# Blockwise attention into a maxout layer on one core: another order of loads, and M computed during batch 0's exps

## The chip, the core and the metric

The kernel runs on one core of one Trainium2 chip. A core has a tensor engine (PE, with its weight loads shown as PEld), a vector engine (DVE), a scalar engine (ACT), GpSimd (POOL) and a sync engine (SP). Each runs its own instructions in order and waits for others by semaphores; 16 DMA engines move data between memory and the on-chip buffer. The metric is the device time of one execution in microseconds, as a median over runs.

## The reference

The input is q, k and v, each 8 batches x 8 heads x 576 positions x 64 in fp32, and three weights. Attention is causal by blocks of 64 positions; its output goes through a layer that takes the larger of two products.

```python
scores = scale * np.matmul(q, k.transpose(0, 1, 3, 2))
mask = (pos[:, None] // 64) >= (pos[None, :] // 64)
attn = softmax(np.where(mask, scores, -1e9))
x = np.matmul(attn, v)            # -> 4608 tokens x 512
g = np.maximum(x @ w1, x @ w2)    # w1, w2: 512 x 1024
out = g @ w_out                   # w_out: 1024 x 512
```

## The kernel before

The maxout is rewritten: max(x w1, x w2) = relu(x (w1 - w2)) + x w2. So the kernel needs D = w1 - w2 (`d_sb`, made by `diff_w`, one fp32 subtraction on DVE for each quarter of 256 columns), h = relu(x D), and M = w2 w_out (`m_sb`), and then out = h w_out + x M. For M, w2 has to be transposed: `bT_unit` does two blocks of 128 columns by eight PE transposes and one copy on DVE into `bT_sb`, and `m_unit` does one of eight 128 x 256 pieces of M by eight matmuls and one copy on DVE.

Attention runs over 32 pairs of heads, four for each batch. Two pairs make a group g; q and k come by group (`load_qk`, fp32, from SP's queue), are cast to bf16 (`cast`, by POOL from the third group on), transposed on PE (`transposes`) and copied out by DVE and ACT. A load that is "gated" is preceded by a tiny memset of POOL on the same buffer, so that SP issues it only when POOL has come to that place in its program. V, w1, w2 and w_out are loaded by POOL's own DMA queue; those to bf16 are cast on the way. w2 is put into stretches of the buffer xT that later batches' x will fill. w1 and w2 are loaded in four quarters each.

Scores go to two PSUM buffers (`ps_s`), ACT takes their exps into `aT`, POOL clears the masked corners (`mask`), and `av` multiplies by V with a column of ones and normalises on DVE (a reciprocal and a multiplication). `x_out` transposes the result into xT. All other PE results share four PSUM buffers (`ps_m`).

The order is written out by hand. Batch 0 (groups 0 and 1, pairs 0 to 3) is cut into small score tiles, `burst_p`, `burst_q1`, `burst_q2`, `burst_q3`, and its av is done in two parts, tiles [0, 1] and [2, 3, 4]. Then comes group 2 (pairs 4 and 5) by `tile_0`, `tile_1`, `tile_2`, each with its exps and masks in `region`, and from group 3 on a loop. Between these stand `fill(n)`, which issues the next steps of a list of units made by `plan()`: h, M, B-transposes and y (the output product, whose PSUM result is copied by DVE for the first two spans of tokens and by ACT later). `fill` counts in matmuls of 512 columns: a transpose step counts 0.25, an M step 0.5, an h step 0.5 in the first span (256 tokens), 0.625 in the second (320 tokens), and a y step 1. In and after the block that closes group 2, `fill_of(g)` spreads what is ready, less 6, over the groups that are left until new tokens come (three groups at g = 2, two at 3, one at 4). `warm_up(n)` issues n matmuls on zeros whose results are not used.

In the list before, a B-transpose unit follows every second h unit of the first span, and M comes after the second span's h.

Each engine's order is that of the program, so a DMA issue of POOL, a cast or a mask delays whatever POOL has to do after it, and a subtraction on DVE delays the copies and relus behind it.

Of the kernel before, what the change touches and what calls it, by code (L numbers as in the profile page):

```python
# [8 lines left out]
FP32 = mybir.dt.float32  # L9
# [5 lines left out]
def kernel(  # L15
# [10 lines left out]
    nc = tc.nc  # L26
# [85 lines left out]
    def load_qk(g, queues, gated=False):  # L112
        b, u = divmod(g, GPB)
        for nm, src, queue in (("q", q, queues[0]), ("k", k, queues[1])):
            if queue is None:
                continue
            raws[nm, g] = t = raw.tile([P, 2, RPP * D], FP32, name=f"{nm}raw")
            if gated:
                nc.gpsimd.memset(t[:, 0, :1], 0.0)
            queue.dma_start(  # L120
                out=t[:],
                in_=src[b, 4 * u:4 * u + 4].rearrange(
                    "(s h) (p t) d -> (h p) s (t d)", h=2, t=RPP),
            )

    def cast(nm, g, parts):
        t = raws[nm, g].rearrange("p s (t d) -> p t s d", d=D)
        if (nm, g) not in qk_n:
            qk_n[nm, g] = qkn.tile([P, RPP, 2, D], BF16, name=f"{nm}n")
        n = qk_n[nm, g]  # L130
        for copy, j0, j1 in parts:
            copy(out=n[:, j0:j1], in_=t[:, j0:j1])  # L132

    def load_v(b, c):
        rows = min(P, S - c * P)
        nc.gpsimd.dma_start(  # L136
            out=vv_r[b % NV][P - rows:, c, :, :D],
            in_=v[b, :, c * P:c * P + rows, :].rearrange("h p d -> p h d"),
        )
# [3 lines left out]
    wor = moe_w_out.rearrange("(c p) f -> p c f", p=P)  # L143

    WB = 256
    w1_raw, w2_sb = {}, []
    for j in range(d_ff // WB):
        row, n = (1, j) if j < 3 else (3, 0)
        t0 = 3 * S - 3 * BLK + n * NDM * WB
        w2_sb.append(xT[:, row, t0:t0 + NDM * WB].rearrange("p (c f) -> p c f", c=NDM))  # L150

    def load_w(j, which=(0, 1)):
        fs = slice(j * WB, (j + 1) * WB)
        if 0 in which:
            w1_raw[j] = wraw.tile([P, NDM, WB], FP32, name="w1raw")
            nc.gpsimd.dma_start(out=w1_raw[j][:], in_=w1r[:, :, fs])
        if 1 in which:
            nc.gpsimd.dma_start(out=w2_sb[j], in_=w2r[:, :, fs])

    def diff_w(j):  # L160
        fs = slice(j * WB, (j + 1) * WB)
        nc.vector.tensor_sub(d_sb[:, :, fs], w1_raw[j][:], w2_sb[j])  # L162

    WH = d_model // 2

    def load_wo(i):
        ds = slice(i * WH, (i + 1) * WH)
        nc.gpsimd.dma_start(out=wo_sb[:, :, ds], in_=wor[:, :, ds])  # L168
# [8 lines left out]
    nc.vector.memset(zeros[:], 0.0)  # L177
    nc.scalar.activation(out=warm[:], in_=warm[:], func=AF.Exp)
    load_qk(1, (SP, SP))
    load_qk(2, (SP, None))  # L180
    make_identity(nc, ident)
    for r in range(NV):
        nc.vector.memset(vv_r[r][:, :, :, D:D + 1], 1.0)
# [6 lines left out]
    cast("k", 0, ((act, 0, 5), (dve, 5, RPP)))  # L190
    for c in range(2):
        load_v(0, c)
    load_w(0, (0,))
    cast("q", 1, ((pool, 7, RPP),))
    cast("k", 1, ((pool, 0, 7),))
    load_w(0, (1,))


    done_tokens = [0]
# [23 lines left out]
    def bT_unit(j):  # L223
        pt = ps_m.tile([P, 2, NDM, P], BF16, name="ps_bT", tag="m")
        for i in range(2):
            for c in range(NDM):
                nc.tensor.transpose(pt[:, i, c, :], w2_sb[j][:, c, i * P:(i + 1) * P], ident[:])
                if i == 1 and c == NDM - 1:
                    nc.vector.tensor_copy(
                        out=bT_sb[:, 2 * j:2 * j + 2, :],  # L230
                        in_=pt.rearrange("p i c d -> p i (c d)"))
                yield

    def m_unit(i, c):
        ds = slice(i * WH, (i + 1) * WH)
        pt = ps_m.tile([P, WH], FP32, name="ps_M", tag="m")
        for f in range(NFF):
            nc.tensor.matmul(  # L238
                pt[:], bT_sb[:, f, c * P:(c + 1) * P], wo_sb[:, f, ds],
                start=(f == 0), stop=(f == NFF - 1),  # L240
            )
            if f == NFF - 1:
                nc.vector.tensor_copy(out=m_sb[:, c, ds], in_=pt[:])
            yield
# [40 lines left out]
    def plan():  # L285
        def h(i, f):
            t0, w = spans[i]
            units.append((h_unit(i, f), t0 + w, w / SPAN, NDM))

        def y(i, s, last=False):  # L290
            t0, w = spans[i]
            if last:
                units.append((y_last(i, s), t0 + w, 0.333, 3 * NY))
            else:
                units.append((y_unit(i, s), t0 + w, 1.0, NY))

        for i in range(NSPAN):
            for f in range(NFF):
                h(i, f)
                if i == 0 and f % 2:  # L300
                    units.append((bT_unit(f // 2), 0, 0.25, 2 * NDM))
                if i > 2 and f % 2 == 0 and f // 2 < tiles[i - 1]:
                    y(i - 1, f // 2)
            if i == 1:
                for n in range(2 * NDM):
                    units.append((m_unit(n // NDM, n % NDM), 0, 0.5, NFF))
                for j in range(2):
                    for s in range(tiles[j]):
                        y(j, s)
        n = tiles[-1]  # L310
        for s in range(n):
            y(NSPAN - 1, s, s == n - 1)
# [21 lines left out]
    def warm_up(n):  # L334
        pw = ps_m.tile([P, SPAN], FP32, name="ps_w", tag="m")
        for _ in range(n):
            nc.tensor.matmul(pw[:], zeros[:, :P], zeros[:], start=True, stop=True)  # L337
# [4 lines left out]
    def transposes(nm, g, copies):  # L342
        n = qk_n.pop((nm, g))
        pts = [ps_m.tile([P, RPP, NP], BF16, name=f"ps_{nm}T", tag="m") for _ in range(2)]
        for j in range(RPP):
            for i in range(2):
                r = slice(i * NP, (i + 1) * NP)
                nc.tensor.transpose(  # L348
                    pts[i][:, j, :], n[r, j].rearrange("p s d -> p (s d)"), ident[r, r],
                )  # L350

        def copy_out(which=(0, 1), part=(0, NP), copy=None):
            p0, p1 = part
            for i in which:
                t = (qT_r if nm == "q" else kT_r)[(2 * g + i) % NT]
                (copy or copies[i])(  # L356
                    out=t[:, p0 * RPP:p1 * RPP].rearrange("q (p j) -> q p j", j=RPP),
                    in_=pts[i][:, :, p0:p1].rearrange("q j p -> q p j"),
                )
        return copy_out  # L360
# [12 lines left out]
    def pad_keys(p):  # L373
        nc.gpsimd.tensor_copy(
            out=kz_r[p % NT].rearrange("p (a c) -> p a c", c=BLK)[:, 0:3:2],
            in_=kT_r[p % NT][:, S - 3 * BLK:].rearrange("p (a c) -> p a c", c=BLK)[:, 0:3:2],
        )
# [31 lines left out]
    def burst_q1(p):  # L409
        burst(p, ((0, QCUT, 320), (1, QCUT, 192)), 384)  # L410

    def burst_q2(p):
        burst(p, ((1, 448, P), (2, QCUT, 320), (4, 512, BLK)), 896)
# [4 lines left out]
    def masks_p(p, eng=None):  # L418
        for a in (0, 256):
            mask(p, a, eng)  # L420

    def masks_q(p, eng=None):
        for a in (1024, 1408):
            mask(p, a, eng)
# [30 lines left out]
    def region(*tiles):  # L455
        for out in tiles:
            out()
# [127 lines left out]
    burst_p(1)  # L585
    warm_up(2)
    masks_p(1)
    for c in range(2, NCH):
        load_v(0, c)
    load_qk(2, (None, SP), gated=True)  # L590
    load_w(1)
    cq = transposes("q", 1, (dve, dve))
    burst_q1(0)
    ck = transposes("k", 1, (dve, dve))
# [15 lines left out]
    masks_p(3, nc.vector)  # L610
    burst_q2(0)
    av(2, [0, 1])
    warm_up(2)
    x_out(0, 0, 2, (act, act))
    av(3, [0, 1])
    diff_w(0)
    burst_q1(1)
    warm_up(2)
    cast("q", 2, ((pool, 0, RPP),))
    masks_q(0)  # L620
    load_w(2)
    burst_q2(1)
    x_out(1, 0, 2)
    warm_up(2)
    burst_q3(1)
    masks_q(1)
    load_w(3)
    fill(4)
    burst_q1(2)
    transposes("q", 2, (dve, act))()  # L630
    burst_q2(2)
    av(0, [2, 3, 4])
    burst_q3(2)
    masks_q(2)
    cast("k", 2, ((pool, 0, RPP),))
    load_wo(0)
    load_wo(1)
    av(1, [2, 3, 4])
    burst_q1(3)
    burst_q2(3)  # L640
    av(2, [2, 3, 4])
    transposes("k", 2, (dve, act))()
    burst_q3(3)
    masks_q(3)
    pad_keys(4)
    pad_keys(5)
    for c in range(NCH):
        load_v(1, c)
    load_qk(3, (SP, SP), gated=True)
    x_out(0, 2, NCH)  # L650
    fill(2)
    diff_w(1)
    outs = tile_0(4), tile_1(4)
    av(3, [2, 3, 4])
    region(*outs)
    x_out(1, 2, NCH)
    fill(4)
    diff_w(2)
    fill(2)
    region(tile_2(4), tile_0(5))  # L660
    fill(4)
    diff_w(3)
    fill(2)
    region(tile_1(5), tile_2(5))
    fill(4)
    fill(2)
    cast("q", 3, ((pool, 0, RPP),))
    cast("k", 3, ((pool, 0, RPP),))
    n = fill_of(GPB)
# [77 lines left out]
```

The softmax here doesn't subtract the row's maximum and nothing guards it: scores larger than these inputs give would overflow.

## Time and profile before

| | |
|---|---|
| median of 3 runs | 265.49 us (264.95 to 265.69) |
| the profiled execution, its own time | 265.55 us |
| its span | 263.7 us |
| PE busy | 250.0 us, 95% of the span |
| DVE, ACT, POOL busy | 137.2, 140.9, 109.9 us |
| HBM read, written | 34.60 MB, 9.44 MB |

The span is what the profiler saw from the first to the last instruction. A busy time is the sum of an engine's instructions; matmuls are pipelined, so their shown lengths overlap. In lines of a timeline the columns are: start in us, length in us, engine, line of the kernel, operation, output and input, count, and in brackets the idle time ahead of it with what ended it. In the table by stretch, the busy time of each engine stands beside its count of instructions.

### The profile page before, as it was taken

What the parts mean: (1) busy time and instruction counts of PE and PEld (TensorE: products, weight loads), DVE (VectorE), ACT (ScalarE), POOL (GpSimd) and SP (SyncE); (2) the same over time, 40 slices, a digit from 0 to 9 for tenths busy, and PEclk for the clock granted to TensorE, in tenths of its full rate; (3) what the DMA queues carried; (4) which work ended last, traced back from release to release, by engine and by line L of the source; (5) the groups of instructions that cost most, each with busy time, mean ns of one, the idle gap of its engine ahead of it and who ended that gap; (6) DMA issues with size and microseconds to landing.
All of it is one profiled execution on the core that took longest, in us unless ns stands there. A gap on an engine that the chain in (4) does not pass through costs nothing.

```text
span 263.7 us, 7204 instructions
## 1 busy us (share of the span) xinstructions
PE 250.0 (95%) x2983; PEld 139.6 (53%) x2983; DVE 137.2 (52%) x301; ACT 140.9 (53%) x198; POOL 109.9 (42%) x274
## 2 busy tenths in 40 slices
PE   8698799999989799999999999999999999999995
PEld 2346566856546455555555555555555544444444
DVE  4867996656668554545454545454544452323200
ACT  2788552676797484848575757575755100111111
POOL 2987914484577647254635563456311000000000
PEclk9999999999999999999999999999999999999999
DMA  7999996689599949986997599679613411112122
GB/s 247 314 218 298 188 234 158 247 94 252 144 182 256 234 68 264 132 252 71 262 150 232 81 227 178 227 82 126 106 42 81 52 66 57 63 58 82 40 95 104
DMA packets 71265, 41.30 MB, mean 157 GB/s; under 512 B 53568, under 2 KB 58048, under 8 KB 71232
## 3 DMA queue, kind: packets, MB, share of 16 engines
q1 hardware_dynamic: 28544, 31.27, 43.2%
q0 software_dynamic: 42272, 8.92, 38.1%
q10 hardware_dynamic: 416, 0.66, 0.7%
q8 instruction: 23, 0.38, 0.6%
q14 instruction: 10, 0.08, 0.1%
HBM read 34.60 MB, written 9.44 MB: 167 GB/s over the span
## 4 chain that ended last, share of the span: by engine, by line
PE 85%; DMA 5%; POOL 3%; ACT 2%; DVE 2%; issue 1%; ACTq 0%; POOLq 0%
PE ps_y L257 35%; PE ps_h L215 21%; PE ps_o L475 10%; PE ps_s L367 7%; PE ps_w L337 3%; DMA qraw<-in_q_dram 3%; PE ps_M L238 3%; PE ps_qT L348 2%; ACT aT L391 2%; DMA xT<-xp 2%; PE ps_kT L348 2%; POOL vv L136 1%; PE ps_y L272 1%; PE ps_s L385 1%; POOL wo_sb L168 1%
## 5 line engine op out<-in xcount | busy, mean ns | idle before, releaser
L391 ACT ACTIVATE aT<-ps_s 128x1024 bf16<-128x1024 f32 (+2 forms) x100 | 95.9, 996 | 28.9 <-PE ps_s L367 26.9
L220 DVE TENSOR_SCALAR g<-ps_h 128x512 bf16<-128x512 f32 (+3 forms) x80 | 50.7, 636 | 63.9 <-PE ps_h L215 62.9
L215 PE MATMUL ps_h<-xT,d_sb 128*128 128x512 bf16 (+3 forms) x320 | 71.7, 358 | 1.8 <-DVE d_sb L162 1.2
L257 PE MATMUL ps_y<-wo_sb,g 128*128 128x512 bf16 x280 | 69.9, 379 | 0.0
L396 POOL MEMSET aT<- 64x128 bf16 x124 | 22.3, 200 | 78.7 <-ACT aT L391 78.0
L475 PEld LDWEIGHTS <-aT 128*128 128x128 bf16 x960 | 37.2, 98 | 14.0 <-issue 2.1
L215 PEld LDWEIGHTS <-d_sb 128*128 128x128 bf16 x320 | 28.7, 98 | 29.7 <-issue 3.5
L262 ACT COPY y<-ps_y 128x512 f32<-128x512 f32 x31 | 18.2, 588 | 48.5 <-PE ps_y L257 45.6
L257 PEld LDWEIGHTS <-g 128*128 128x128 bf16 x280 | 25.7, 98 | 30.0 <-issue 2.6
L475 PE MATMUL ps_o<-vv,aT 128*128 128x65 bf16 x960 | 39.7, 194 | 0.0
L257 PE MATMUL ps_y<-m_sb,xT 128*128 128x512 bf16 x140 | 37.9, 380 | 0.0
L367 PE MATMUL ps_s<-qT,kT 64*128 64x64 bf16 (+6 forms) x344 | 31.4, 280 | 3.9 <-ACT aT L447 1.6
L136 POOL DMA_DIRECT2D vv<-in_v_dram x40 | 33.7, 848 | 1.6 <-issue 1.2
L482 DVE TENSOR_TENSOR xp<-ps_o,rec 128x256 bf16<-128x256 f32 (+1 forms) x64 | 31.4, 491 | 2.2
L481 DVE RECIPROCAL rec<-ps_o 128x4 f32<-128x4 f32 (+1 forms) x64 | 12.1, 189 | 35.4 <-PE ps_o L475 34.9
L356 ACT COPY qT<-ps_qT 128x576 bf16<-128x576 bf16 (+1 forms) x17 | 10.3, 614 | 24.8 <-PE ps_qT L348 24.8
L257 PEld LDWEIGHTS <-xT 128*128 128x128 bf16 x140 | 12.9, 98 | 16.0 <-issue 3.0
L132 POOL CAST qn<-qraw 128x1152 bf16<-128x1152 f32 (+1 forms) x16 | 16.9, 1058 | 8.6 <-DMA qraw<-in_q_dram 8.6
L367 PEld LDWEIGHTS <-kT 64*128 64x128 bf16 x344 | 12.3, 94 | 13.7 <-issue 8.2
L207 POOL COPY g<-g 128x512 bf16<-128x512 bf16 x8 | 4.9, 613 | 31.5 <-DVE g L220 30.9
L132 POOL CAST kn<-kraw 128x1152 bf16<-128x1152 f32 (+1 forms) x15 | 17.1, 1139 | 1.1 <-DMA kraw<-in_k_dram 1.0
L356 ACT COPY kT<-ps_kT 128x576 bf16<-128x576 bf16 x15 | 9.6, 639 | 10.5 <-PE ps_kT L348 10.0
(57 smaller groups left out, 161.8 us busy)
## 6 DMA issues: line engine op xcount, KB each, us to landing
qraw<-in_q_dram SPq DMA_DIRECT2D x16, 576.0 KB, 4.8
out_dram<-y SPq DMA_DIRECT2D x35, 256.0 KB, 2.6
kraw<-in_k_dram SPq DMA_DIRECT2D x15, 576.0 KB, 6.0
vv<-in_v_dram POOLq DMA_DIRECT2D x32, 128.0 KB, 6.0
w1raw<-in_moe_w_dram POOLq DMA_DIRECT2D x4, 512.0 KB, 7.8
xT<-in_moe_w_dram POOLq DMA_DIRECT2D x4, 256.0 KB, 8.5
wo_sb<-in_moe_w_out_dram POOLq DMA_DIRECT2D x2, 512.0 KB, 8.1
kraw<-in_k_dram ACTq DMA_DIRECT2D x1, 576.0 KB, 5.6
```

Of the source, the lines that this page charges most:

```text
L132: copy(out=n[:, j0:j1], in_=t[:, j0:j1])
L136: nc.gpsimd.dma_start(out=vv_r[b % NV][P - rows:, c, :, :D], in_=v[b, :, c * P:c * P + rows, :].rearrange("h p d -> p h d"),)
L215: nc.tensor.matmul(pt[:, :w], d_sb[:, c, f * P:(f + 1) * P], xT[:, c, t0:t0 + w], start=(c == 0), stop=(c == NDM - 1),)
L220: nc.vector.tensor_scalar_max(g[:, f, m:m + w], pt[:, :w], 0.0)
L257: nc.tensor.matmul(py[:], lhs, rhs, start=(n == 0), stop=(n == len(terms) - 1),)
L262: (dve if i < 2 else act)(out=y[:], in_=py[:])
L356: (copy or copies[i])(out=t[:, p0 * RPP:p1 * RPP].rearrange("q (p j) -> q p j", j=RPP), in_=pts[i][:, :, p0:p1].rearrange("q j p -> q p j"),)
L367: nc.tensor.matmul(ps[:, hh, col:col + w], kT[r, k0:k0 + P], qT[r, q0:q0 + w], start=True, stop=True,)
L391: nc.scalar.activation(out=aT_r[p % NA][:, :, a0:a0 + w], in_=ps[:, :, :w], func=AF.Exp, scale=scale,)
L396: (eng or nc.gpsimd).memset(aT_r[p % NA][BLK:, :, a0:a0 + BLK], 0.0)
L475: nc.tensor.matmul(po[:, gi, hh, :], a[:, hh, a0:a0 + P], vv[:, c, h0 + 2 * hh, :], start=(mm == 0), stop=(mm == n_mm - 1),)
L482: nc.vector.tensor_mul(xp[:, :, ts[0]:ts[0] + n, p % 2].rearrange("q s t d -> q t s d"), po[:, :, :, :D], rec[:, :n].to_broadcast([P, n, 2 ...
```

## The change

Loads. w2 comes in two halves of 512 columns and not in four quarters, both early, with none of w1 ahead of them. The third q is no longer loaded at the start. Then come the first half of w_out, the late chunks of V, the second half of w_out and all four quarters of w1, all issued by POOL after the masks of pair 1. The third group's q and k are loaded together after the masks of pair 2.

Units. The B-transposes and M stand at the head of the list, ahead of all h.

Order. Three `warm_up(2)` of batch 0 become `fill(2)`, more fills stand between batch 0's bursts, its second av parts come later, the subtractions come after, and group 2 starts behind all of h's first span.

```diff
+    WC = d_ff // 2
+    w2_sb = [
+        xT[:, row, 3 * S - 3 * BLK:3 * S - 3 * BLK + NDM * WC].rearrange("p (c f) -> p c f", c=NDM)
+        for row in (1, 3)]
+    def load_w1(j):
+        w1_raw[j] = wraw.tile([P, NDM, WB], FP32, name="w1raw")
+        nc.gpsimd.dma_start(out=w1_raw[j][:], in_=w1r[:, :, j * WB:(j + 1) * WB])
+    def load_w2(i):
+        nc.gpsimd.dma_start(out=w2_sb[i], in_=w2r[:, :, i * WC:(i + 1) * WC])
     def diff_w(j):
-        fs = slice(j * WB, (j + 1) * WB)
-        nc.vector.tensor_sub(d_sb[:, :, fs], w1_raw[j][:], w2_sb[j])
+        n = j * WB % WC
+        nc.vector.tensor_sub(
+            d_sb[:, :, j * WB:(j + 1) * WB], w1_raw[j][:], w2_sb[j * WB // WC][:, :, n:n + WB])
...
     load_qk(1, (SP, SP))
-    load_qk(2, (SP, None))
...
-    load_w(0, (0,))
+    load_w2(0)
     cast("q", 1, ((pool, 7, RPP),))
     cast("k", 1, ((pool, 0, 7),))
-    load_w(0, (1,))
+    load_w2(1)
...
+        for n in range(NFF // 2):
+            units.append((bT_unit(n), 0, 0.25, 2 * NDM))
+        for n in range(2 * NDM):
+            units.append((m_unit(n // NDM, n % NDM), 0, 0.5, NFF))
         for i in range(NSPAN):
             for f in range(NFF):
                 h(i, f)
-                if i == 0 and f % 2:
-                    units.append((bT_unit(f // 2), 0, 0.25, 2 * NDM))
...
             if i == 1:
-                for n in range(2 * NDM):
-                    units.append((m_unit(n // NDM, n % NDM), 0, 0.5, NFF))
...
     masks_p(1)
+    load_wo(0)
     for c in range(2, NCH):
         load_v(0, c)
-    load_qk(2, (None, SP), gated=True)
-    load_w(1)
+    load_wo(1)
+    for j in range(d_ff // WB):
+        load_w1(j)
...
     av(2, [0, 1])
-    warm_up(2)
+    fill(2)
     x_out(0, 0, 2, (act, act))
     av(3, [0, 1])
-    diff_w(0)
     burst_q1(1)
-    warm_up(2)
-    cast("q", 2, ((pool, 0, RPP),))
+    fill(2)
     masks_q(0)
-    load_w(2)
     burst_q2(1)
     x_out(1, 0, 2)
-    warm_up(2)
+    fill(2)
     burst_q3(1)
     masks_q(1)
-    load_w(3)
-    fill(4)
+    fill(2)
     burst_q1(2)
-    transposes("q", 2, (dve, act))()
     burst_q2(2)
-    av(0, [2, 3, 4])
+    fill(4)
+    fill(4)
     burst_q3(2)
     masks_q(2)
-    cast("k", 2, ((pool, 0, RPP),))
-    load_wo(0)
-    load_wo(1)
-    av(1, [2, 3, 4])
+    load_qk(2, (SP, SP), gated=True)
     burst_q1(3)
+    fill(4)
+    fill(4)
     burst_q2(3)
-    av(2, [2, 3, 4])
-    transposes("k", 2, (dve, act))()
+    av(0, [2, 3, 4])
     burst_q3(3)
     masks_q(3)
+    for c in range(NCH):
+        load_v(1, c)
+    av(1, [2, 3, 4])
+    x_out(0, 2, NCH)
+    av(2, [2, 3, 4])
+    fill(4)
+    diff_w(0)
+    av(3, [2, 3, 4])
+    fill(4)
+    x_out(1, 2, NCH)
+    fill(8)
+    diff_w(1)
+    cast("q", 2, ((pool, 0, RPP),))
+    cast("k", 2, ((pool, 0, RPP),))
+    load_qk(3, (SP, SP), gated=True)
+    fill(4)
+    diff_w(2)
+    fill(4)
+    transposes("q", 2, (dve, act))()
+    diff_w(3)
+    fill(4)
+    transposes("k", 2, (dve, act))()
     pad_keys(4)
     pad_keys(5)
-    for c in range(NCH):
-        load_v(1, c)
-    load_qk(3, (SP, SP), gated=True)
-    x_out(0, 2, NCH)
-    fill(2)
-    diff_w(1)
-    outs = tile_0(4), tile_1(4)
-    av(3, [2, 3, 4])
-    region(*outs)
-    x_out(1, 2, NCH)
-    fill(4)
-    diff_w(2)
-    fill(2)
+    fill(4)
+    region(tile_0(4), tile_1(4))
+    fill(5)
     region(tile_2(4), tile_0(5))
-    fill(4)
-    diff_w(3)
-    fill(2)
+    fill(10)
     region(tile_1(5), tile_2(5))
-    fill(4)
-    fill(2)
+    fill(5)
     cast("q", 3, ((pool, 0, RPP),))
     cast("k", 3, ((pool, 0, RPP),))
     n = fill_of(GPB)
```

More of the change, by code (lines that the diff above doesn't have):

```diff
@@ L145 @@
     WB = 256
[L146 to L152, printed above, removed]
-        fs = slice(j * WB, (j + 1) * WB)
[L154 to L158, printed above, removed]
+    w1_raw = {}
+    WC = d_ff // 2
[7 more added lines that the diff above has]
+        nc.gpsimd.dma_start(out=w2_sb[i], in_=w2r[:, :, i * WC:(i + 1) * WC])
     def diff_w(j):
-        fs = slice(j * WB, (j + 1) * WB)
-        nc.vector.tensor_sub(d_sb[:, :, fs], w1_raw[j][:], w2_sb[j])
+        n = j * WB % WC
+        nc.vector.tensor_sub(
+            d_sb[:, :, j * WB:(j + 1) * WB], w1_raw[j][:], w2_sb[j * WB // WC][:, :, n:n + WB])
     WH = d_model // 2
@@ L225, in bT_unit @@
         for i in range(2):
+            f = 2 * j + i
             for c in range(NDM):
-                nc.tensor.transpose(pt[:, i, c, :], w2_sb[j][:, c, i * P:(i + 1) * P], ident[:])
+                nc.tensor.transpose(pt[:, i, c, :], w2_sb[f // (NFF // 2)][:, c, f % (NFF // 2) * P:(f % (NFF // 2) + 1) * P], ident[:])
                 if i == 1 and c == NDM - 1:
@@ L612 @@
     av(2, [0, 1])
-    warm_up(2)
+    fill(2)
     x_out(0, 0, 2, (act, act))
     av(3, [0, 1])
-    diff_w(0)
     burst_q1(1)
-    warm_up(2)
-    cast("q", 2, ((pool, 0, RPP),))
+    fill(2)
     masks_q(0)
-    load_w(2)
     burst_q2(1)
     x_out(1, 0, 2)
-    warm_up(2)
+    fill(2)
     burst_q3(1)
     masks_q(1)
-    load_w(3)
+    fill(2)
+    burst_q1(2)
+    burst_q2(2)
     fill(4)
-    burst_q1(2)
-    transposes("q", 2, (dve, act))()
-    burst_q2(2)
-    av(0, [2, 3, 4])
+    fill(4)
     burst_q3(2)
     masks_q(2)
-    cast("k", 2, ((pool, 0, RPP),))
-    load_wo(0)
-    load_wo(1)
-    av(1, [2, 3, 4])
+    load_qk(2, (SP, SP), gated=True)
     burst_q1(3)
+    fill(4)
+    fill(4)
     burst_q2(3)
-    av(2, [2, 3, 4])
-    transposes("k", 2, (dve, act))()
+    av(0, [2, 3, 4])
     burst_q3(3)
     masks_q(3)
+    for c in range(NCH):
[20 more added lines that the diff above has]
+    transposes("k", 2, (dve, act))()
     pad_keys(4)
     pad_keys(5)
-    for c in range(NCH):
-        load_v(1, c)
-    load_qk(3, (SP, SP), gated=True)
-    x_out(0, 2, NCH)
-    fill(2)
-    diff_w(1)
-    outs = tile_0(4), tile_1(4)
-    av(3, [2, 3, 4])
-    region(*outs)
-    x_out(1, 2, NCH)
     fill(4)
-    diff_w(2)
-    fill(2)
+    region(tile_0(4), tile_1(4))
+    fill(5)
     region(tile_2(4), tile_0(5))
-    fill(4)
-    diff_w(3)
-    fill(2)
+    fill(10)
     region(tile_1(5), tile_2(5))
-    fill(4)
-    fill(2)
+    fill(5)
     cast("q", 3, ((pool, 0, RPP),))
```

## The prediction

> **What bounds the kernel now.** I read the busy shares of the page first, then busy time by stretch of time, then the tensor engine's (PE's) own timeline and waits, then the other engines' timelines in the stretches that the change touches. The table by stretch (columns: stretch in us, its length, busy us and instructions of PE, weight loads, DVE, ACT, POOL, PE clock, DMA share, GB/s):
>
> ```profile
> 8.00:17.20 9.20, 6.58 (x127) 3.37 (x121) 7.09 (x20) 7.46 (x12) 8.76 (x17) 1.00 1.67 241
> 17.20:24.00 6.80, 6.57 (x125) 4.27 (x124) 5.25 (x12) 5.94 (x10) 4.25 (x11) 1.00 1.21 286
> 24.00:32.00 8.00, 6.00 (x128) 4.50 (x127) 6.51 (x14) 4.80 (x7) 7.84 (x15) 1.00 1.32 223
> 32.00:41.00 9.00, 7.38 (x88) 5.49 (x88) 7.99 (x15) 4.25 (x6) 2.56 (x9) 1.00 1.63 223
> 45.24:56.90 11.66, 11.66 (x196) 8.48 (x197) 6.56 (x17) 7.56 (x10) 6.39 (x20) 1.00 0.79 195
> 56.90:68.00 11.10, 11.10 (x182) 6.41 (x175) 6.62 (x15) 7.56 (x10) 6.15 (x15) 1.00 1.01 187
> 76.20:90.00 13.80, 11.26 (x162) 6.24 (x162) 8.30 (x18) 10.61 (x14) 10.96 (x31) 1.00 1.50 194
> ```
>
> From 45.24 us, where the scores of pair 6 (group 3) start, PE has no gap for 22 us, and later few. So a microsecond of PE work taken out of groups 3 and 4 is a microsecond gained, provided that it is done earlier in PE time now idle. How much is idle? On PE's timeline after 16.26 us (before that the two programs give PE the same work) there are seven gaps: 0.23, 0.25, 0.24, 1.26, 0.63, 0.59, 0.56, in all 3.76 us. Add the three pairs of dummy matmuls that go; they stand in the chain of waits:
>
> ```profile
> 16.26 0.43 PE ps_w L337 x2
> 17.53 0.54 PE ps_w L337 x2
> 18.51 0.54 PE ps_w L337 x2
> ```
>
> That is 1.51 us. So 5.3 us is all that the early stretch can give. Two of the gaps are waits for the w1-w2 subtraction, which DVE does between other things (DVE's timeline):
>
> ```profile
> 31.19 1.22 DVE L162 TENSOR_TENSOR d_sb<-w1raw,xT 128x1024 bf16<-128x1024 f32 x1
> 32.33 0.68 DVE L229 COPY bT_sb<-ps_bT 128x1024 bf16<-128x1024 bf16 x1
> 33.11 0.86 DVE L220 TENSOR_SCALAR g<-ps_h 128x256 bf16<-128x256 f32 x2
> 33.89 1.22 DVE L162 TENSOR_TENSOR d_sb<-w1raw,xT 128x1024 bf16<-128x1024 f32 x1
> ```
>
> DVE is nearly without a pause from 26.9 to 40.4: while the h matmuls start, it is as much the bound as PE. Last, what a group with little filler looks like: group 6, after 4 units of filler, on PE and on ACT:
>
> ```profile
> 76.17 0.39 PE L367 MATMUL ps_s<-qT,kT 64*128 64x512 bf16 x2 [0.32 <-DVE g L220]
> 77.39 0.39 PE L367 MATMUL ps_s<-qT,kT 64*128 64x64 bf16 x4 [0.82 <-ACT aT L447]
> ```
> ```profile
> 75.09 1.95 ACT L391 ACTIVATE aT<-ps_s 128x1024 bf16<-128x1024 f32 x2
> 77.06 0.27 ACT L447 ACTIVATE aT<-ps_s 64x128 bf16<-64x128 f32 x1
> ```
>
> The new scores need the two score buffers, which the last exps of the group before still read until 77.33.
>
> [...] the trace has 1.216. So the four subtractions cost 4.9 us of DVE wherever they stand. [...] the trace shows the engines full from 2 to 41 us. [...] The first 16 dummies took 0.40 us each here, later ones 0.22[...]
>
> **The change, part by part.**
> Filler. One unit is a 512-column matmul. Before, 24 units are handed out by hand, then n=32 in the block that ends batch 0, then 31 and 31 in groups 3 and 4. After, the hand-placed fills sum to 76 of the 124 ready (8 B-transposes, 32 M, 16 and 20 h, 48 y), so n = (48-6)/3 = 14, and groups 3 and 4 get 14 each. Before, groups 3 and 4 held 39 M matmuls at 0.118 (12 in 1.42) and 42.5 units of y at 0.217 (6 in 1.30): 13.8 us; after, 28 of y: 6.1. So 7.7 us of PE work moves ahead of pair 6. Without any idle, pair 6 would start at 45.24 - 3.76 - 1.51 + 7.7 = 47.7.
>
> Loads. Landings before, by issue: V's first chunk 11.9, w1's first quarter 14.6, w2's 16.1; then steps of 1.4 (w1 quarter), 1.35 (w2 quarter), 2.65 (w_out half), 1.0 to 1.2 (V chunk). With the third q out of the start (1.45 us of full DMA rate) I put V's first at 10.5, w2's halves at 14.4 and 17.1, w_out's first at 19.8, late V by 22.8, w_out's second at 25.5, and w1 with the third q, k (issued about 23.5, behind the masks of pair 2) between 27 and 34. Needed: w2's second half at 18.6, w_out at 20.6 and 29.2, w1 at 30.5 to 39. All in time, by 0.8 us at the tightest (w_out's first half). POOL's issues (two of w_out at 0.88, four of w1 at 0.77) push the masks of pair 0 to 19, needed at 25: free.
>
> Walking PE from 16.26: bursts, four B-transposes in the dummies' places (0.54 each), M in two pairs of 0.95 at 20.6 and 23.0. The last exp of batch 0 ends near 26.8 (before: 26.6), since ACT loses two q/k copies but waits for PE. Now the idle that I find:
> - x_out of group 0 right behind pair 1's last product: reciprocal 0.20 + multiply 0.56 + hand-overs, 0.85.
> - x_out of group 1: DVE has the first subtraction ahead of pair 3's reciprocal, 0.5.
> - h columns 2,3 wait for the second subtraction (behind the last M copies, about 35.15 to 36.3): 0.7.
> - h 4,5: third subtraction, behind two relus: 0.9. h 6,7: fourth one, behind two relus and the q copy; then the k copy before pair 4's scores: 1.25. Check: from 34.8 DVE must do 3 x 1.14 + 3 x 0.68 (relus) + 2 x 0.67 + an M copy 0.35 = 7.15 us against 4.3 of PE's. This ends at 42.0.
> - The second score buffer, when pair 5 starts: 0.3.
> - POOL casts the fourth q only after pair 5's masks, which wait for its exps: scores end at 47.2, masks at 49.3, cast 50.5, PE there at 49.9: 0.65.
> Sum 5.15, so pair 6 starts at 47.7 + 5.15 = 52.8, 7.6 later; that eats the 7.7.
>
> Afterwards. (a) The fifth q is loaded behind the fourth k's cast (51.6), lands after 3.85 and is cast in 1.15: 56.9. With 14 units PE wants it 2.8 us after pair 6 starts, at 55.7 (before: 3.5 us after, at 48.76, with 1.1 to spare): +1.2. (b) The starts of groups 4 and 5. At group 6, from the end of the last scores (74.81) to 77.71 passed 2.90 us; with only 2 units (0.43), x_out (0.33) and the new scores (0.54) inside, 1.6 is idle, twice: +3.2. Before, 12 units stood there and nothing waited. From group 5 on the filler is the same as before.
>
> Sum against the profiled run (265.55: span 263.7 and 1.85 around it; median 265.49): +7.6 - 7.7 + 1.2 + 3.2 = +4.3, so 269.8.
>
> **Bounds of what the trace doesn't show.** [...] Sharing between w1 and the third q, k: at worst w1's last quarter lands at 36, still before 39: 0. Should w_out's first half be late, PE stops ahead of pair 2's last exps, one for one: 0 to +3. The DVE run: 1.5 to 4 us against my 2.85, since the order of hand-overs is by estimate. Starts of groups 4 and 5: 0 to 1.8 each. [...]
>
> **Rivals.**
> 1. PE stays full until pair 6 (faster): the fills cover every gap, T0 is 47.7, and even with (a) and (b) the end is 265.5 - 5.3 + 4.4 = 264.6. It decides from a pair-6 start of 48.5 on downwards. For it: filler stands in nearly every place where PE waited before. Against: 7.15 us of DVE work in a row. 8%.
> 2. The starts of groups 4 and 5 are hidden (ACT early enough): 269.8 - 3.2 = 266.6. Against it: group 6's rows. 15%.
> 3. The load order turns on the change: w_out or w1 late, M stalls inside the exps instead of filling them, so the change doesn't do what it says. +2 to +4 more: 272.8. For it: DMA full to 41 us and a margin of 0.8. 17%.
> 4. Mine, 60%: own range 267.8 to 271.6.
>
> **How the numbers follow.** No change is what lies within 0.3% (0.8 us), about what a measurement of this kernel tells. Faster: most of rival 1, 7%. Same: its rest and the edge of rival 2, 8%. Slower: 85%. The range 266.2 to 272.8 leaves out rival 1, the low edge of rival 2 and the upper half of rival 3.
>
> **What would show it.** M matmuls between 20 and 34 us; no ps_w after 16.3; pair 6's scores at 52 to 54; waits of ps_h for d_sb of over 2 us in all; POOL's cast of the fourth q behind masks; PE gaps of over 1 us at the starts of groups 4 and 5, released by L447 of ACT. It is wrong if pair 6 starts before 49, or if PE waits for wo_sb's DMA.

## The result, and the profile after

The changed kernel takes 271.62 us (271.25 to 272.01) against 265.41 before in the same comparison: a ratio of 1.0236, 95% interval 1.0215 to 1.0257. It is 6.2 us slower; forecast were 4.3, with 266.2 to 272.8 as the range. A repetition on another chip (e10) gave 1.0223 (1.0194 to 1.0253). In what follows, experiments on the changed kernel are set against 1.023, the mean of the two, and 1% is 2.65 us.

The profiled execution has a span of 270.2 us (263.7 before). PE's busy time is what it was (250.3 against 250.0), so the time is idle time. The table by stretch, with the columns of the prediction:

```profile
17.20:24.00 6.80, 5.73 (x82) 4.16 (x82) 4.11 (x10) 4.93 (x9) 2.43 (x8) 1.00 1.96 174
24.00:32.00 8.00, 7.12 (x146) 6.12 (x143) 4.71 (x13) 2.84 (x4) 4.36 (x10) 1.00 1.08 355
32.00:41.00 9.00, 6.29 (x85) 4.80 (x84) 7.98 (x16) 0.64 (x1) 2.97 (x5) 1.00 1.72 163
41.00:55.17 14.17, 11.96 (x136) 6.48 (x131) 8.44 (x17) 8.28 (x11) 4.32 (x14) 1.00 0.22 68
55.17:80.00 24.83, 21.84 (x412) 13.53 (x413) 15.17 (x36) 19.31 (x26) 16.09 (x43) 1.00 1.02 245
```

From 24 to 32 us PE is fuller than before (7.12 of 8 us, it was 6.00): M does fill the time of batch 0's last exps. From 32 to 41 us PE has 6.29 of 9 us where it had 7.38, and from 55.17 on, where groups 3 and 4 had run without a gap, it has 21.84 of 24.83. DVE is as full from 32 to 41 us as before (7.98 us, it was 7.99), but ACT has 0.64 us to do where it had 4.25. PE's gaps of over half a microsecond up to 75 us, from its timeline (idle time and what ended it in brackets):

```profile
21.77 1.92 PE L238 MATMUL ps_M<-wo_sb,bT_sb 128*128 128x256 bf16 x16 [1.07 <-DMA wo_sb<-in_moe_w_out_dram]
...
29.02 0.20 PE L513 MATMUL ps_xe<-ident,xp 64*128 64x64 bf16 x1 [0.88 <-DVE xp L482]
...
33.41 0.20 PE L513 MATMUL ps_xe<-ident,xp 64*128 64x64 bf16 x1 [0.73 <-DVE xp L482]
...
37.27 1.05 PE L214 MATMUL ps_h<-xT,d_sb 128*128 128x256 bf16 x8 [0.78 <-DVE d_sb L161]
...
39.88 1.03 PE L214 MATMUL ps_h<-xT,d_sb 128*128 128x256 bf16 x8 [1.20 <-DVE g L219]
...
42.04 1.03 PE L214 MATMUL ps_h<-xT,d_sb 128*128 128x256 bf16 x8 [0.75 <-ACT kT L356]
...
52.55 0.43 PE L348 MATMUL ps_qT<-ident,qn 64*128 64x64 bf16 x18 [0.75 <-POOL qn L132]
...
58.76 0.44 PE L348 MATMUL ps_qT<-ident,qn 64*128 64x64 bf16 x18 [0.67 <-POOL qn L132]
...
65.31 0.40 PE L367 MATMUL ps_s<-qT,kT 64*128 64x64 bf16 x4 [0.82 <-ACT aT L447]
...
74.49 0.39 PE L367 MATMUL ps_s<-qT,kT 64*128 64x64 bf16 x4 [0.82 <-ACT aT L447]
```

DVE's timeline says why h starts so haltingly: from the second subtraction on (the first is at 31.45), the subtractions (L161), the relus (L219) and a copy of q (L356) follow each other without a break.

```profile
35.99 1.22 DVE L161 TENSOR_TENSOR d_sb<-w1raw,xT 128x1024 bf16<-128x1024 f32 x1
37.12 0.75 DVE L219 TENSOR_SCALAR g<-ps_h 128x256 bf16<-128x256 f32 x2
37.79 1.70 DVE L161 TENSOR_TENSOR d_sb<-w1raw,xT 128x1024 bf16<-128x1024 f32 x1
39.41 0.74 DVE L219 TENSOR_SCALAR g<-ps_h 128x256 bf16<-128x256 f32 x2
40.08 0.74 DVE L356 COPY qT<-ps_qT 128x576 bf16<-128x576 bf16 x1
40.74 1.21 DVE L161 TENSOR_TENSOR d_sb<-w1raw,xT 128x1024 bf16<-128x1024 f32 x1
```

PE's early work starts up to 0.8 us apart from run to run, so I count from the three dummy matmuls ahead of pair 2 (12.60 before, 12.79 after, 11.97 to 12.29 in the experiments). Pair 6 starts 32.64 us later before and 42.38 after: 9.74 us lost. From pair 6 to the first filler of group 5 (68.51 before, 74.81 after) it is 23.27 against 19.64: 3.63 won back. Together 6.1; from there on the two profiles run in parallel, but for 0.3 us at a transposing transfer near 96 us.

### The profile page after: what moved, and what is told of

Its sections match the earlier page's. It is cut to its first block, busy times and chain, and to the rows that moved or that the text cites. A ratio compares the mean times of both kernels' runs of the same rounds, so it can differ in the third digit from the quotient of the medians.

```text
span 270.2 us, 7184 instructions
## 1 busy us (share of the span) xinstructions
PE 250.3 (93%) x2977; PEld 138.7 (51%) x2977; DVE 137.4 (51%) x301; ACT 141.1 (52%) x198; POOL 108.1 (40%) x273
## 2 busy tenths in 40 slices
DMA packets 70209, 41.30 MB, mean 153 GB/s; under 512 B 53536, under 2 KB 56992, under 8 KB 70176
## 3 DMA queue, kind: packets, MB, share of 16 engines
HBM read 34.60 MB, written 9.44 MB: 163 GB/s over the span
## 4 chain that ended last, share of the span: by engine, by line
PE 75%; DMA 10%; ACT 5%; DVE 4%; POOL 2%; issue 2%; SPq 0%; ACTq 0%; POOLq 0%
PE ps_y L257 32%; PE ps_h L214 20%; PE ps_o L475 9%; PE ps_s L367 6%; ACT aT L391 4%; DMA wo_sb<-in_moe_w_out_dram 4%; DMA kraw<-in_k_dram 3%; PE ps_M L238 2%; DVE d_sb L161 2%; DMA xT<-xp 2%; PE ps_qT L348 2%; DMA qraw<-in_q_dram 1%; PE ps_kT L348 1%; PE ps_y L272 1%; DVE g L219 1%
## 5 line engine op out<-in xcount | busy, mean ns | idle before, releaser
L219 DVE TENSOR_SCALAR g<-ps_h 128x512 bf16<-128x512 f32 (+3 forms) x80 | 50.3, 635 | 66.1 <-PE ps_h L214 64.4
L475 PEld LDWEIGHTS <-aT 128*128 128x128 bf16 x960 | 37.3, 98 | 14.7 <-issue 1.8
L356 ACT COPY qT<-ps_qT 128x576 bf16<-128x576 bf16 (+1 forms) x17 | 10.3, 614 | 33.4 <-PE ps_qT L348 33.4
L356 ACT COPY kT<-ps_kT 128x576 bf16<-128x576 bf16 x15 | 9.6, 638 | 9.8 <-PE ps_kT L348 8.8
## 6 DMA issues: line engine op xcount, KB each, us to landing
wo_sb<-in_moe_w_out_dram POOLq DMA_DIRECT2D x2, 512.0 KB, 11.4
```

The lines of the kernel that those rows point to most:

```text
L219: nc.vector.tensor_scalar_max(g[:, f, m:m + w], pt[:, :w], 0.0)
L356: (copy or copies[i])(out=t[:, p0 * RPP:p1 * RPP].rearrange("q (p j) -> q p j", j=RPP), in_=pts[i][:, :, p0:p1].rearrange("q j p -> q p j"),)
L475: nc.tensor.matmul(po[:, gi, hh, :], a[:, hh, a0:a0 + P], vv[:, c, h0 + 2 * hh, :], start=(mm == 0), stop=(mm == n_mm - 1),)
```

## The experiments

Theory: filler taken out of groups 3 and 4 is lost again, partly before pair 6 (to DVE's order, to POOL's order and to w_out's landing) and partly at the starts of groups 4 and 5, which then wait for exps. Rivals: those starts are hidden; the transfers alone are the cause; the waits lie on one chain, so that mending one moves the loss.

**e1: only the filler moved, on the kernel before.**

```diff
-    n = fill_of(GPB)
+    n = fill_of(GPB) + 34
```

> The kernel before with one number changed: 34 units of filler more in the block that closes group 2, so that groups 3 and 4 keep 14 units each as in the changed kernel; loads, units and all else as before. Theory (the filler taken out of groups 3 and 4 leaves their ends waiting for exps, 1.6 us at the starts of groups 4 and 5): pair 6 starts 7.4 us later, two new gaps of 0.3 + 0.8 us appear at the starts of groups 4 and 5, the time rises by 3.2 us (2.4 to 3.6). Rival (those starts are hidden by ACT, the loss lies wholly in the stretch before pair 6): 0, within 0.5 us.

267.38 us, ratio 1.0083 (1.0061 to 1.0104): 2.2 us slower. PE's timeline of e1 at the starts of groups 4 and 5:

```profile
60.71 0.40 PE L367 MATMUL ps_s<-qT,kT 64*128 64x64 bf16 x4 [0.82 <-ACT aT L447]
...
69.90 0.40 PE L367 MATMUL ps_s<-qT,kT 64*128 64x64 bf16 x4 [0.82 <-ACT aT L447]
```

These are the gaps of the changed kernel, made with the loads and the units of before. The stretch from pair 6 (51.30) to group 5's filler (70.22) is 18.92 us, 4.35 shorter than before where 7.7 us of work are gone: 3.35 lost at two starts. That is the size forecast for the two starts. The total of 2.2 is below the 3.2, and below the range given for it, because the same filler closes a gap of 0.56 us before the fourth q and more on the way: pair 6 starts 6.65 us later, not 7.4. The starts are not hidden: that rival falls. Nor are the transfers alone the cause, since none is changed here.

**e2: relus of the first span on ACT, on the changed kernel.**

```diff
-                nc.vector.tensor_scalar_max(g[:, f, m:m + w], pt[:, :w], 0.0)
+                if i == 0:
+                    nc.scalar.activation(out=g[:, f, m:m + w], in_=pt[:, :w], func=AF.Relu)
+                else:
+                    nc.vector.tensor_scalar_max(g[:, f, m:m + w], pt[:, :w], 0.0)
```

> The changed kernel with the eight relus of the first token span on ACT, which has nothing to do from 27.8 to 38.8 us, in place of DVE. Theory (between the last M copies and pair 4's scores DVE is the bound: subtractions, relus and copies in a row): the PE gaps of 0.78, 1.20, 0.75 and 0.26 us there shrink to 1.2 or so in all, pair 6 starts and the kernel ends 1.6 us earlier (1.0 to 2.2). Rival (the subtractions wait for w1's landing, or the exps set the end of the stretch): under 0.4 us.

270.22 us, ratio 1.0193 (1.0170 to 1.0216), 1.0 us faster than the changed kernel. Its interval touches that of the changed kernel and overlaps that of its repetition, so by time alone the gain is barely clear of noise; it rests on the gaps. PE's gaps and DVE in that stretch:

```profile
36.91 1.05 PE L214 MATMUL ps_h<-xT,d_sb 128*128 128x256 bf16 x8 [0.78 <-DVE d_sb L161]
...
38.99 1.05 PE L214 MATMUL ps_h<-xT,d_sb 128*128 128x256 bf16 x8 [0.67 <-DVE d_sb L161]
...
40.79 1.05 PE L214 MATMUL ps_h<-xT,d_sb 128*128 128x256 bf16 x8 [0.39 <-DVE d_sb L161]
```

```profile
35.63 3.30 DVE L161 TENSOR_TENSOR d_sb<-w1raw,xT 128x1024 bf16<-128x1024 f32 x2
```

The gaps fall from 2.99 us (0.78, 1.20, 0.75, 0.26) to 1.84, and what is left waits for the subtractions alone. So DVE was the bound there. The gaps that the profile of the changed kernel puts down to a relu and to ACT's copy of k (1.20 and 0.75) are the 0.67 and 0.39 here. The gain is 1.15 by the gaps, not 1.6: two subtractions that should take 2.4 us took 3.30, while POOL cast the third k (36.19 to 37.86).

**e3: POOL casts the fourth q, k and admits the fifth before pair 5's last masks.**

```diff
+    cast("q", 3, ((pool, 0, RPP),))
+    cast("k", 3, ((pool, 0, RPP),))
+    load_qk(4, (SP, SP), gated=True)
     region(tile_1(5), tile_2(5))
     fill(5)
-    cast("q", 3, ((pool, 0, RPP),))
-    cast("k", 3, ((pool, 0, RPP),))
...
-    pool_work(4)
```

> The changed kernel with the casts of the fourth q, k and the gated load of the fifth q, k put before the last scores of pair 5, so that on POOL they stand ahead of pair 5's last masks. Theory (the transposes of the fourth and fifth q wait for POOL's place in its order, not for data): the gaps of 0.75 and 0.67 us before those transposes go, 1.4 us faster (1.0 to 1.6). Rival (the masks, now later, hold up something else, or the exps set these places anyway): 0 to 0.4 us faster.

269.26 us, ratio 1.0168 (1.0139 to 1.0198): 1.6 us faster than the changed kernel. POOL's timeline, first of the changed kernel, then of e3:

```profile
50.94 0.34 POOL L396 MEMSET aT<- 64x128 bf16 x2 [0.72 <-ACT aT L391]
51.35 1.14 POOL L132 CAST qn<-qraw 128x1152 bf16<-128x1152 f32 x1
```

```profile
47.84 1.14 POOL L132 CAST qn<-qraw 128x1152 bf16<-128x1152 f32 x1
48.93 1.14 POOL L132 CAST kn<-kraw 128x1152 bf16<-128x1152 f32 x1
```

Both gaps (0.75 and 0.67) are gone from PE's timeline. The data had been there all along: the fourth q had landed at 43.6 (issued 38.49, 5.1 us).

**e4: without the load of w2's second half**, so half of w2 is left out.

```diff
-    load_w2(1)
...
     make_identity(nc, ident)
+    nc.vector.memset(w2_sb[1], 0.0)
```

> The changed kernel without the load of w2's second half (its place is cleared by DVE at the start instead, so half of w2 is left out of the result), which takes about 2.5 us of transfers from ahead of w_out's first half. Theory (M's first matmuls wait 1.07 us for w_out, and PE is full from there to the end of batch 0's products): the gap at 20.7 us goes and the end comes 1.0 us earlier (0.6 to 1.3). Rival (later waits for DVE take up what is gained): 0 to 0.3 us.

270.17 us, ratio 1.0178 (1.0152 to 1.0204): 1.4 us faster, a little over the range of its theory. M starts right behind the bursts with no gap:

```profile
19.82 1.92 PE L238 MATMUL ps_M<-wo_sb,bT_sb 128*128 128x256 bf16 x16
```

Counted from the dummies that is 7.84 us instead of 8.98. The later gaps for DVE are about as in the changed kernel (0.88, 0.90, 0.78, 1.21, 0.75; the second was 0.73). So the wait for w_out is paid in full at the end.

**e5: on the kernel before, filler held back for groups 5 and 6.** If a group's end needs filler, then the kernel before has the same fault at groups 6 and 7.

```diff
-        return -(-max(0, ready() - KEEP) // left)
+        return -(-max(0, ready() - (22 if g < 5 else KEEP)) // left)
```
(the edit is to the last line of `fill_of`, in its form with `left`)

> The kernel before with one number changed: while the first two batches' tokens are all there is (groups 2 to 4), 22 units of filler are held back in place of 6, so groups 2, 3 and 4 get about 26 each and groups 5 and 6 about 24 in place of 16. Theory (a group's end needs some 2 us of filler behind its last scores, whichever group it is): the gaps at the starts of groups 6 and 7, 1.5 us each, shrink to 0.6 or less, and the time falls by 1.8 us (1.0 to 2.5). Rival (those gaps come from ACT's total load, so filler only moves them): within 0.5 us.

263.46 us, ratio 0.9942 (0.9925 to 0.9959): 1.5 us faster than the kernel before, and the fastest of all with e6. PE at the starts of groups 6 and 7:

```profile
74.70 0.40 PE L367 MATMUL ps_s<-qT,kT 64*128 64x64 bf16 x4 [0.35 <-ACT aT L447]
...
84.77 0.40 PE L367 MATMUL ps_s<-qT,kT 64*128 64x64 bf16 x4 [0.35 <-ACT aT L447]
```

The gaps of 0.32 + 0.82 are down to 0.35 each. ACT has the same work as before, so it is where the filler stands, not how much ACT has to do, that makes these gaps.

**e6: e5 with the mends for DVE and for the fourth q.** To e5's and e2's edits come these:

```diff
+    load_qk(3, (SP, SP), gated=True)
     for c in range(NCH):
         load_v(1, c)
-    load_qk(3, (SP, SP), gated=True)
...
-    diff_w(1)
     outs = tile_0(4), tile_1(4)
     av(3, [2, 3, 4])
+    diff_w(1)
```

> The kernel of e5 (the kernel before with 22 units held back) with three edits for the waits that the experiments on the changed kernel sized: first-span relus on ACT, the second subtraction behind pair 3's normalisation, and the fourth q, k loaded ahead of the second batch's V. Theory (in this stretch PE waits for DVE's order and for the fourth q): the gaps of 1.26, 0.63, 0.59 and 0.56 us shrink to 1.0 in all, the time falls by another 2 us, to 261.5 (260.5 to 262.5). Rival (what DVE is relieved of, PE then waits for elsewhere, for w1 or q): as e5, within 0.5 us.

263.75 us, ratio 0.9944 (0.9923 to 0.9965): no gain over e5. The miss is plain on PE's timeline of e6:

```profile
28.51 0.20 PE L516 MATMUL ps_xe<-ident,xp 64*128 64x64 bf16 x1 [0.88 <-DVE xp L485]
...
29.64 1.05 PE L215 MATMUL ps_h<-xT,d_sb 128*128 128x256 bf16 x8 [0.79 <-DVE d_sb L162]
...
34.02 0.23 PE L388 MATMUL ps_s<-qT,kz 64*128 64x64 bf16 x4 [0.56 <-ACT aT L394]
...
37.10 2.47 PE L215 MATMUL ps_h<-xT,d_sb 128*128 128x320 bf16 x17 [0.69 <-ACT g L221]
...
47.42 0.44 PE L351 MATMUL ps_qT<-ident,qn 64*128 64x64 bf16 x18 [0.69 <-POOL qn L132]
```

They sum to 3.61 us; in e5 the gaps here are 1.26, 0.63, 0.60 and 1.18, 3.67. In this order ACT has exps of pairs 4 and 5 to do just when it gets the relus, so PE waits for ACT where it waited for DVE, then for the fifth q. This is what the rival said.

**e7: e2 and e3 together**, on the changed kernel.

> The changed kernel with the edits of e2 and e3 together. Theory (two separate causes, in a row on PE's path): the gains add up, 1.2 + 1.8 = 2.9 us against the changed kernel, 268.7 (268.2 to 269.2). Rival (both shorten one chain, and the longer of the two is what counts): 269.3 or more.

268.16 us, ratio 1.0124 (1.0089 to 1.0159): 2.8 us faster than the changed kernel; e2 and e3 alone gave 1.0 and 1.6. Within the interval, which is 0.9 us wide to each side, they add up, as separate waits in a row do. Its executions lie far apart (266.71 to 269.76). The profile is of the shortest and shows no wait for w_out at all: w2's halves and w_out's first half landed 14.7, 17.3 and 19.9 us after the start, against 16.2, 18.7 and 21.7 in the changed kernel's profile. PE's early work, the dummies included, was 0.7 us ahead there too, so w_out came 1.1 us earlier for PE, which is the whole wait. The two edits have no part in this.

**e8: e3 with the 14 units left to groups 3 and 4** (n = 0 in the block that closes group 2, the fifth q admitted before `region(tile_2(4), tile_0(5))`).

> The kernel of e3 with the 14 units of filler that closed group 2 left to groups 3 and 4 (21 each in place of 14), and the fifth q, k loaded before pair 5's first exps. Theory (filler is worth more behind the last scores of groups 3 and 4 than ahead of pair 6): pair 6 starts 3 us earlier, the gaps at the starts of groups 4 and 5 shrink from 1.6 to 0.5 us each, 2.0 us faster than e3 (1.2 to 2.4), 267.2. Rival (ahead of pair 6 PE now waits for the fourth q or for exps instead): within 0.5 us of e3.

267.96 us, ratio 1.0111 (1.0091 to 1.0132): 1.5 us faster than e3 (1.8 by the profiles, from the dummies to group 5's filler). On PE's timeline of e8:

```profile
51.12 0.61 PE L367 MATMUL ps_s<-qT,kT 64*128 64x512 bf16 x6 [0.91 <-DVE kT L356]
...
60.94 0.40 PE L367 MATMUL ps_s<-qT,kT 64*128 64x64 bf16 x4 [0.26 <-ACT aT L447]
...
70.56 0.40 PE L367 MATMUL ps_s<-qT,kT 64*128 64x64 bf16 x4 [0.26 <-ACT aT L447]
```

The two starts wait 0.26 instead of 0.34 + 0.82; of this, 0.91 goes to a new wait for the copy of the fourth k, which the filler had hidden. So e8 falls 0.5 us short of its point, within its range.

**e9: the mends together**: e2 and e8, M's copies on ACT, 12 units held back.

> The changed kernel with every mend found: the edits of e2 and e8 together, M's copies on ACT too, and 12 units held back for groups 5 and 6 (18 units each in groups 3 and 4, 19 in 5 and 6). Theory (the causes are separate and add up): 1.1 us off e8 for the relus, 0.7 for the copies (the second x_out no longer waits behind DVE), 0.3 for what is held back: 265.9 (265.0 to 266.8), level with the kernel before and above e5's 263.5, since loads and DVE still hold PE up ahead of pair 4. Rival (ACT's new work delays exps of batch 0, which then are the bound): 267.5 or more.

266.49 us, ratio 1.0038 (1.0016 to 1.0061); the executions behind the ratio run from 264.8 to 268.5. The profile is of the longest of these (268.51), 2 us above the median. In it the second x_out waits 0.23 us instead of 0.73 and the waits for the subtractions are gone, but a new one stands in their place:

```profile
39.51 0.44 PE L351 MATMUL ps_kT<-ident,kn 64*128 64x64 bf16 x18 [2.01 <-POOL kraw L119]
...
50.96 0.61 PE L370 MATMUL ps_s<-qT,kT 64*128 64x512 bf16 x6 [0.85 <-ACT kT L359]
...
60.78 0.40 PE L370 MATMUL ps_s<-qT,kT 64*128 64x64 bf16 x4 [0.82 <-ACT aT L450]
```

The third k, issued at 24.64, needs 12.9 us to land, among w1 and V, and is cast from 37.67 to 39.45. In this execution, with DVE out of the way, the landing of k is the bound; whether the median execution waits as long is not shown. The last line shows that one mend undoes another. With 12 units held back, only 3 of filler stand behind the last scores of groups 3 and 4, where e8 has 6, and the wait of 0.82 us is back. So e9 is not the best that these mends can give. That the changed order cannot get below the kernel before is not shown; no run here did.

**e10: the changed kernel again.**

> The changed kernel once more, on the same chip as e9, for the spread of its wait for w_out. Theory (that wait is a matter of when transfers land, within a microsecond, and the rest is set by the order): between 270.5 and 272; the gap before the first M between 0.5 and 1.2 us, all other gaps as in its first profile within 0.1 us.

271.31 us, ratio 1.0223. The wait for w_out is 1.10 us; the other gaps are within 0.1 us of the first profile except two: the wait at h columns 4 and 5 is 1.00 instead of 1.20, and there is a new wait of 0.39 for w2 at the first B-transposes. The first of these goes with the subtraction beside POOL's cast of k, 1.50 us here against 1.70.

## Why the prediction was right, and where it was off

The direction, the mechanism and the order of size were right, and the result lies inside the range, but 1.8 us above the point and just above the 271.6 that ended its own likeliest case. One of its own signs of being wrong came true, PE waiting for w_out's transfer, and pair 6 started at 55.2 where it had 52 to 54. The prediction's sum by its terms, in us:

| term | forecast | measured |
|---|---|---|
| w_out's first half late | 0 (margin 0.8) | 1.07 |
| x_out of group 0 | 0.85 | 0.88 |
| x_out of group 1 | 0.5 | 0.73 |
| h 2,3 | 0.7 | 0.78 |
| h 4,5 | 0.9 | 1.20 |
| h 6,7 and the k copy | 1.25 | 0.75 + 0.26 |
| second score buffer | 0.3 | 0.35 |
| fourth q's cast | 0.65 | 0.75 |
| idle before pair 6 | 5.15 | 6.77 |
| pair 6 later by | 7.6 | 9.74 |
| fifth q | 1.2 | 0.67 |
| starts of groups 4 and 5 | 3.2 | 3.2 |
| from pair 6 to group 5 | -3.3 | -3.63 |

- **The filler's account** (7.7 us out of groups 3 and 4) and **the starts of groups 4 and 5** held: from the end of the last scores to the next filler pass 2.88 and 2.87 us, with 1.30 of work inside, so 1.6 idle at each, as forecast. e1 shows that this needs nothing of the new load order; e5 and e8 undo it from both sides. The profiles together show how much filler a start needs. With 2 to 4 matmuls of 512 columns behind the last scores PE waits 0.82 us for the last exps (changed kernel, e1, e9 and group 6 before), with 6 or 7 it waits 0.26 to 0.35 (e8, e5), and with 8 (e5's group 5) or 12 (before, group 4) not at all.
- **The DVE run** held in place and size, 2.99 against 2.85 for its three terms. e2 shows that the relus are part of the bound. That the subtractions cost 4.9 us wherever they stand did not hold: the third took 1.70 us beside POOL's cast, and the four 5.35.
- **POOL's place** for the fourth and fifth q held in place. The fifth was over-priced by half, because pair 6 itself started late; e3 removes both.
- **The step that failed is the landing of w_out's first half.** I put it at 19.8 by adding one step per transfer; it came at 21.7 (11.61 + 10.1). Most of this is the first half of w2: it landed 4.2 us behind V's second chunk (12.0 to 16.2), where I had about 2.7. V's first chunk was 0.2 us ahead of my time, w2's second half took 2.5 us, and w_out 3.0 where I had 2.65. So part of rival 3 came true, at 1.07 us instead of 2 to 4, and the margin of 0.8 us was never there. e4 shows that this wait is paid in full. In the profiles with the changed kernel's loads the wait is anything from 0 (e7) through 0.55 (e8) and 0.86 (e3) to 1.10 (e10), and the step of w2's first half, 4.2 us in the changed kernel, is 3.3 in e7 (11.4 to 14.7). Why it varies by so much with the same loads, and why it is not 2.7 in either, is open.
- **What remains**, about 0.5 us of the 9.74, is not in any of these gaps. About 0.3 of it stands in h's first span, whose four groups of eight matmuls take 4.02 us where they took 3.71 before. The rest I did not follow. (The three pairs of dummies come to 1.61 us and not 1.51: on PE's timeline the first starts at 16.09.) A loss of clock is not part of it: the granted clock is 1.00 in all five stretches.
- **Errors that offset.** The fifth q, over-priced by 0.5 us, made up for a part of what w_out's landing added. Without this the result would have been near 272, still inside the range but further from the point.
- **Rival 1** (PE full until pair 6) never came near: it needed a start before 48.5 and got 55.2. **Rival 2** falls by e1.
- **The bytes** are the same in either order of loads: 34.60 MB read from HBM and 41.30 MB moved, in both profiles.

## What to carry to other kernels

Filler has a best place, not only an amount. Ahead of a wait it is worth up to the length of the wait; here, moved from a place where it hid exps to a stretch where DVE was the bound, it lost more than it gained. Before pulling work into the idle time of one engine, add up what each engine has to do in that stretch, in its own order; here the forecast's sum gave DVE 7.15 us of work where PE had 4.3. And once a mechanism is sized, look for it in the version that you meant to leave alone: the cheapest gain of this study (e5, 0.6%) is one number in the kernel before.

## What the runs showed of the hardware

- **DVE and POOL hold each other up.** A subtraction of two buffers takes 1.22 us alone and 1.50 to 1.89 where POOL's cast of k was under way when it began (1.50 in e3 and e10, 1.70 in the changed kernel, 1.89 in e8), and the cast 1.14 alone and up to 2.18 (e10). From e10, DVE first, then POOL:

```profile
37.59 1.50 DVE L161 TENSOR_TENSOR d_sb<-w1raw,xT 128x1024 bf16<-128x1024 f32 x1
```

```profile
35.84 2.18 POOL L132 CAST kn<-kraw 128x1152 bf16<-128x1152 f32 x1 [1.05 <-DMA kraw<-in_k_dram]
```

  In e10 the cast ends at 38.02 and the subtraction at 39.09, 1.07 us later, and in the changed kernel (38.42 and 39.49) and e8 (37.34 and 38.41) the distance is 1.07 too, though the subtraction took 1.50, 1.70 and 1.89 us. So in these it got almost nothing done until the cast was over.
- **POOL's DMA issues can wait for landings.** With nothing but issues in its way, POOL stood still for 1.66 and 2.27 us in the changed kernel:

```profile
18.99 0.75 POOL L154 DMA_DIRECT2D w1raw<-in_moe_w_dram  x1 [1.66 <-DMA xT<-in_moe_w_dram]
22.01 0.75 POOL L154 DMA_DIRECT2D w1raw<-in_moe_w_dram  x1 [2.27 <-DMA wo_sb<-in_moe_w_out_dram]
```

  Each time eight earlier loads of its queue were under way, and it went on 0.3 us after the oldest had landed (18.7 and 21.7). At the same two issues it stood still for 1.48 and 2.25 us in e10 and for 0.70 and 1.91 in e8. Whether the limit is the chip's or the program's was not tried. It cost nothing here, since the last mask ahead of the next loads waited 0.91 us for exps anyway.
